# Seventeen completion waits at the end of a kernel, in GpSimd's program or in SyncE's

## The chip, the cores and the metric

The kernel runs on one core of one Trainium2 chip. The core has five engines with a program each: TensorE (PE, matrix products), VectorE (DVE), ScalarE (ACT), GpSimd (POOL) and SyncE (SP, which computes nothing; it issues transfers and waits). The engines meet only through semaphores: an instruction may wait until a semaphore has reached a value, and an instruction or a finished transfer may raise one. The metric is the device time of one launch in microseconds (us), as the median of several runs.

## What is computed

One block over 2048 tokens of width 448: a layer norm, a linear attention with 16 heads of 28 columns, a dense layer pair with a squared relu (448 to 1792 to 448), and a gate that joins the two. Inputs and output are bfloat16. Cut to its core:

```python
xn = _layernorm(x)
q, k, v = split(xn @ wqkv)                      # 16 heads of 28 columns
pq, pk = phi(q), phi(k)                         # where(t > 0, t + 1, exp(t)) + 1e-6
kv = einsum("bhsd,bhse->bhde", pk, v);  z = einsum("bhsd->bhd", pk)
s = (einsum("bhqd,bhde->bhqe", pq, kv) / (einsum("bhqd,bhd->bhq", pq, z) + 1e-6)) @ wo
r = relu(xn @ w1 + b1)
g = silu((r * r) @ w2 + b2)
return x + s * g
```

## The kernel before

The tokens stand in sixteen tiles of 128 rows. The kernel loads `x` and the weights, normalises the tiles, turns them on TensorE or by transfers, and then streams matrix products: keys, queries and the first dense layer tile by tile, then the token sums of the attention, the second dense layer (gate) and the attention's output. The result of a tile is put together in `gbuf` by VectorE and leaves with one transfer to `out`.

No engine's program is written down directly. `Program.add` collects operations with what they read and write; `schedule` puts them in an order for each engine, with durations that the code estimates; `emit` then writes each engine's program. For every operation `emit` works out which semaphores it has to wait for, and the inner function `body(h)` (made by `body_of(e)`) issues them in order: first `h.wait_ge(...)` for each wait, then the operation, which raises its engine's own semaphore by 1 or, when it is a transfer (`op.nbytes` is not 0), a semaphore of its own by 16.

Seventeen transfers write `out`: fourteen whole tiles (in `s_unit`, 112 KB each, twelve of them issued by SP and those of tiles 2 and 3 by ACT), and the last two tiles by `gate_last` (tile 14 whole by SP; tile 15 as a left part of 256 columns by ACT and a right part of 192 columns by SP, which is issued last of all). Line 429 is the helper `dma` that issues every transfer. Nothing in the kernel reads `out`, so something has to hold the launch open until the seventeen have landed. That is the loop at lines 297 to 300, at the end of `body`: one engine waits for each of the seventeen semaphores to reach 16. Line 295 is the wait that stands ahead of an operation anywhere else.

GpSimd has little to do here: it fills constants in the first 7.4 us (masks, an identity), and at line 1278 it scales a 128x64 piece of a weight. All its later candidates (the additions named `ad..`) were given to VectorE by the scheduler.

Of the kernel before, what the change touches and what calls it, by code (L numbers as in the profile page):

```python
# [46 lines left out]
class Program:  # L47
# [200 lines left out]
    def emit(self, nc, es):  # L248
        sems = {e: es.enter_context(nc.semaphore("q_" + e)) for e in self.ENGINES}
        n_dma = 0  # L250
        groups = {}
        for e in self.ENGINES:
            k = 0
            for op in self.order[e]:
                if op.group is not None:
                    if op.group not in groups:
                        groups[op.group] = es.enter_context(nc.semaphore(f"d{n_dma}")), ("d", n_dma)
                        n_dma += 1
                    op.sem, op.key = groups[op.group]
                    op.seq = 16 * sum(o.group == op.group for o in self.ops)  # L260
                elif op.nbytes:
                    op.sem, op.seq, op.key = es.enter_context(nc.semaphore(f"d{n_dma}")), 16, ("d", n_dma)
                    n_dma += 1
                elif op.label.startswith("table"):
                    op.sem, op.seq, op.key = es.enter_context(nc.semaphore(op.label)), 1, op.label
                else:
                    k += 1
                    op.sem, op.seq, op.key = sems[e], k, e
        done = {}
        waits = {}  # L270
        prev = {}
        for op in sorted(self.ops, key=lambda o: (o.start, 0 if o.eng == "pe" else 1)):
            e = op.eng
            known = dict(prev.get(e, {}))
            need = []
            deps = set(op.deps) | set(self.bankdeps.get(op, ()))
            deps.discard(op)
            for d in sorted(deps, key=lambda d: -d.end):
                if d.key == e == "pe" and d is not op.sync:
                    continue  # L280
                if known.get(d.key, 0) >= d.seq:
                    continue
                need.append((d.sem, d.seq))
                for kk, vv in done[d].items():
                    if known.get(kk, 0) < vv:
                        known[kk] = vv
                known[d.key] = max(known.get(d.key, 0), d.seq)
            waits[op] = need
            prev[e] = known
            done[op] = known  # L290
        def body_of(e):
            def body(h):
                for op in self.order[e]:
                    for s, v in waits[op]:
                        h.wait_ge(s, v)
                    op.emit(h, e).then_inc(op.sem, 16 if op.nbytes else 1)
                if e == "sp":
                    for o in self.ops:
                        if o.nbytes and o.writes and o.writes[0][0] == "out":
                            h.wait_ge(o.sem, 16)  # L300

            return body

        for e, h in (("sp", nc.sync), ("act", nc.scalar), ("pe", nc.tensor), ("dve", nc.vector), ("pool", nc.gpsimd)):
            body_of(e)(h)
# [1089 lines left out]
```

## Time and profile before

| what | value |
|---|---|
| time, median of 3 runs | 143.82 us (143.81 to 143.93) |
| the profiled execution: its own time | 144.04 us |
| the profiled execution: span from the program's first to its last instruction | 142.5 us |
| time outside the span | 1.54 us |
| TensorE busy | 138.5 us, 97% of the span |
| VectorE, ScalarE busy | 103.1 us, 79.0 us |
| GpSimd busy | 6.7 us, 40 instructions |
| granted TensorE clock | full in all slices |

The page lists the instructions of the program alone. Waits are instructions too (`EVENT_SEMAPHORE`); they are not counted as busy. A "q" behind an engine's name means its sequencer, that is waits and issued transfers. The trace also records every update of a semaphore with its time, before and after the program's own instructions; times here count from the first instruction of the program.

### The profile page before, as it was taken

The numbers are of one execution on the slowest core, as the hardware profiler recorded it, in microseconds if no ns is written. First come the engines' busy times: TensorE is split into PE (matmuls) and PEld (weight loads), VectorE is DVE, ScalarE is ACT, GpSimd is POOL, SyncE is SP. The second block draws the span as 40 slices with busy tenths as digits, with TensorE's granted clock in tenths as the row PEclk, the third lists the DMA queues.
The fourth block names the chain that finished last, engine by engine and source line by source line (L and its number), as shares of the span: only waits on it lengthen the run. The fifth ranks groups of instructions, "written<-read, shape, count | busy, mean of one in ns | idle before, by whom it ended". The sixth has DMA issues, their size and how long they took to land.

```text
span 142.5 us, 3235 instructions
## 1 busy us (share of the span) xinstructions
PE 138.5 (97%) x1300; PEld 71.2 (50%) x1300; DVE 103.1 (72%) x222; ACT 79.0 (55%) x146; POOL 6.7 (5%) x40
## 2 busy tenths in 40 slices
PE   7899999999999999999999999999999999999992
PEld 7854445454444544444544444435547455555472
DVE  2747999779689897789777799876035516874875
ACT  3578898040779626697863757787139430301412
POOL 7900001000000000000000000000000000000000
PEclk9999999999999999999999999999999999999999
DMA  4999994239933100233000000000686000223033
GB/s 94 312 302 292 338 293 78 44 49 270 212 42 49 20 0 0 46 50 47 9 5 0 0 0 5 0 0 18 155 223 145 1 0 17 93 88 101 32 97 97
DMA packets 23500, 12.91 MB, mean 91 GB/s; under 512 B 14274, under 2 KB 22718, under 8 KB 23486
## 3 DMA queue, kind: packets, MB, share of 16 engines
q1 hardware_dynamic: 21470, 11.17, 31.3%
q10 hardware_dynamic: 2016, 1.54, 4.7%
q8 instruction: 10, 0.16, 0.5%
q14 instruction: 4, 0.03, 0.1%
HBM read 9.23 MB, written 1.90 MB: 78 GB/s over the span
## 4 chain that ended last, share of the span: by engine, by line
PE 92%; DMA 3%; DVE 2%; SPq 1%; issue 0%
PE pb L780 29%; PE pb L1086 22%; PE pb L1178 7%; PE pb L881 7%; PE pb L723 7%; PE pb L733 6%; PE pb L1103 4%; DMA w_k<-in_A_wqkv_dram 3%; PE pb L1143 3%; PE pb L860 1%; DVE gbuf L1167 1%; PE pb L887 1%; PE pb L823 1%; PE pb L795 1%; PE pb L1030 1%; SPq L429 1%
## 5 line engine op out<-in xcount | busy, mean ns | idle before, releaser
L780 PE MATMUL pb<-xT,w 64*128 64x512 bf16 x378 | 43.6, 376 | 0.0
L1086 PE MATMUL pb<-w,r 64*128 64x448 bf16 x336 | 34.6, 349 | 0.0
L758 ACT ACTIVATE r<-pb,b1f 128x512 bf16<-128x512 f32 x40 | 25.7, 685 | 14.3 <-PE pb L780 13.9
L780 PEld LDWEIGHTS pb<-xT,w 64*128 64x128 bf16 x378 | 18.3, 94 | 21.8
L1086 PEld LDWEIGHTS pb<-w,r 64*128 64x128 bf16 x336 | 16.2, 94 | 16.0 <-issue 0.4
L770 ACT ACTIVATE r<-r 128x1024 bf16<-128x1024 bf16 x15 | 15.7, 1062 | 0.3
L755 DVE TENSOR_SCALAR r<-pb,b1f 128x512 bf16<-128x512 f32 x16 | 11.7, 745 | 4.1 <-PE pb L780 4.0
L1198 DVE TENSOR_TENSOR gbuf<-pb,gbuf 128x448 bf16<-128x448 f32 x14 | 8.1, 618 | 6.7 <-PE pb L1178 6.7
L490 DVE BATCH_NORM_STATS2 st<-x_tok 128x6 f32<-128x448 bf16 x16 | 9.6, 614 | 3.2 <-DMA x_tok<-in_A_x_dram 3.2
L723 PE MATMUL pb<-w_k,xT 64*128 64x448 bf16 x98 | 11.5, 349 | 0.0
L733 PE MATMUL pb<-xT,w_q 64*128 64x512 bf16 x84 | 11.0, 376 | 0.0
L1126 ACT ACTIVATE gbuf<-gbuf 128x448 bf16<-128x448 bf16 x14 | 7.0, 570 | 6.5 <-DVE gbuf L1076 5.9
L1178 PE MATMUL pb<-w_k,pqT 64*128 64x448 bf16 x96 | 10.6, 349 | 0.0
L1076 DVE TENSOR_TENSOR gbuf<-pb,b2b 128x448 bf16<-128x448 f32 x14 | 8.0, 614 | 3.4 <-PE pb L1086 2.0
L994 DVE TENSOR_TENSOR pqT<-pqT,xT 128x2048 bf16<-128x2048 bf16 x3 | 3.7, 1222 | 8.3 <-DMA xT<-scr 8.3
L713 DVE SCALAR_TENSOR_TENSOR pk<-pb,pk 128x448 bf16<-128x448 f32 x16 | 9.5, 617 | 0.2
L881 PE MATMUL pb<-pk,xn 128*128 128x448 bf16 x48 | 9.6, 353 | 0.0
L701 ACT ACTIVATE pk<-pb 128x448 bf16<-128x448 f32 x16 | 7.8, 543 | 3.1 <-PE pb L723 2.5
L701 ACT ACTIVATE pqT<-pb 128x512 bf16<-128x512 f32 x12 | 6.5, 597 | 4.9 <-PE pb L733 4.9
L769 DVE TENSOR_TENSOR r<-r 128x1024 bf16<-128x1024 bf16 x13 | 8.6, 685 | 0.1
L917 DVE TENSOR_TENSOR zacc<-zacc,pk 128x448 f32<-128x448 f32 x13 | 8.0, 618 | 0.1
L520 DVE TENSOR_SCALAR xn<-x_tok,mv,rstd 128x448 bf16<-128x448 bf16 x16 | 7.5, 500 | 0.6 <-ACT rstd L502 0.3
(98 smaller groups left out, 134.5 us busy)
## 6 DMA issues: line engine op xcount, KB each, us to landing
w<-in_B_w_dram SPq DMA_DIRECT2D x1, 1568.0 KB, 11.2
out_dram<-gbuf SPq DMA_DIRECT2D x13, 112.0 KB, 1.7
x_tok<-in_A_x_dram SPq DMA_DIRECT2D x3, 448.0 KB, 6.3
xT<-gbuf SPq DMA_DIRECT2D x32, 32.0 KB, 2.0
w<-in_B_w_dram SPq DMA_DIRECT2D x2, 384.0 KB, 6.3
xT<-scr SPq DMA_DIRECT2D x6, 112.0 KB
w<-in_B_w_dram SPq DMA_DIRECT2D x1, 576.0 KB, 5.8
xT<-scr ACTq DMA_DIRECT2D x5, 112.0 KB
```

The lines of the kernel that those rows point to most:

```text
L490: add("dve", lambda e, _: e.bn_stats(st6[:, si, :], x_tok[:, si, :]), [("x", si)], [("st", si)], 0.61, label=f"bn{si}").prio = hp(si, 0)
L701: "act", lambda e, _: e.activation(out=slot, in_=ps(buf)[0:rows, 0:n], func=AF.Exp), [buf, "actw"],
L713: lambda e, _: e.scalar_tensor_tensor(out=slot, in0=ps(buf)[0:rows, 0:n], scalar=1.0 + 1e-6, in1=slot, op0=ALU.add, op1=ALU.max),
L723: return e.matmul(ps(b)[:, 0:D], x_tile(rows, si, c), w_k[rows, c, :], start=start, stop=stop)
L733: return e.matmul(ps(b)[:, 0:512], w_q[rows, c, m * P : (m + 1) * P], x_group(rows, g, c), start=start, stop=stop,)
L755: return e.tensor_scalar(out=slot, in0=ps(b)[:, 0:512], scalar1=b1f[:, fi : fi + 1], scalar2=0.0, op0=ALU.add, op1=ALU.max)
L758: return e.activation(out=slot, in_=ps(b)[:, 0:512], func=AF.Relu, bias=b1f[:, fi : fi + 1])
L770: return e.activation(out=both, in_=both, func=AF.Square)
L780: return e.matmul(ps(b)[:, 0:512], w_1[rows, c, fi * P : (fi + 1) * P], x_group(rows, g, c), start=start, stop=stop,)
L881: last = e.matmul(ps(b)[:, 0:D], xn_cols(si, c * P, (c + 1) * P), pk[:, si, :], start=(si == 0), stop=(si == NT - 1),)
L1086: return e.matmul(ps(b)[:, 0:D], r_cols(rows, fi, si), w_2[rows, fi, :], start=start, stop=stop)
L1178: return e.matmul(ps(b)[:, 0:D], w, msb[rows, c, :], start=start, stop=stop)
```

## The change

One word in `emit`: the loop over the seventeen transfers is written at the end of GpSimd's program, and no longer at the end of SyncE's.

```diff
@@ -294,7 +294,7 @@
                     for s, v in waits[op]:
                         h.wait_ge(s, v)
                     op.emit(h, e).then_inc(op.sem, 16 if op.nbytes else 1)
-                if e == "sp":
+                if e == "pool":
                     for o in self.ops:
                         if o.nbytes and o.writes and o.writes[0][0] == "out":
                             h.wait_ge(o.sem, 16)
```

In the built program the seventeen waits are nine instructions in both kernels, with the same pairs in the same order: the first holds one wait, the other eight two each. The last two of the nine hold the wait for ACT's left part of tile 15 and, at the very end, that for SP's right part. On SP the nine stood behind the issue of the last transfer; on GpSimd they stand behind the scaling at line 1278. All other instructions are the same on each engine, in the same order.

## The prediction

> **What bounds the kernel now.** I read the page's busy times, then the chain that ended last in order of time, then the result transfers, then the waits of SP and GpSimd, and last the semaphore updates behind the program. The first view says that TensorE fills the span, so only what comes before its first or after its last product could be shortened or lengthened by other engines. The chain (start us, us, what) shows how the work ends.
>
> ```profile
> PE 138.5 (97%) x1300; PEld 71.2 (50%) x1300; DVE 103.1 (72%) x222; ACT 79.0 (55%) x146; POOL 6.7 (5%) x40
> ```
>
> ```profile
> 134.46 4.30 PE pb L1143 x28
> ...
> 140.16 0.48 DVE gbuf L1167 x2
> 140.65 0.02 issue
> 140.67 0.26 DVE gbuf L1167
> ```
>
> The last computation is VectorE's addition that ends at 140.93. From there to the span's end at 142.5 no engine computes: it is the last result transfer. Next are the lines of the result transfers (duration min/median/max in ns, first and last start in us), their issue to landing, and the nine wait instructions.
>
> ```profile
> L429 SPq DMA_DIRECT2D out_dram<-gbuf x14: 332/333/441, 120.1 to 141.0; - x14
> L429 ACTq DMA_DIRECT2D out_dram<-gbuf x3: 338/368/372, 125.7 to 140.5; - x3
> ```
>
> ```profile
> out_dram<-gbuf ACTq DMA_DIRECT2D x1, 64.0 KB, 1.6
> out_dram<-gbuf SPq DMA_DIRECT2D x1, 48.0 KB, 1.5
> ```
>
> ```profile
> L300 SPq EVENT_SEMAPHORE  x9: 17/28/28, 141.3 to 142.5; - x9
> ```
>
> ```profile
> SPq L300 <- DMA out_dram<-gbuf: 0.7, 2, 0.3
> ```
>
> SP issues the last transfer at 140.96 and is free of it at 141.29. Seven of the nine waits are already fulfilled and run through, some 60 ns apart, until 141.75. The eighth is held until ACT's 64 KB have landed at 142.08, the ninth until SP's 48 KB have landed: that semaphore's last update is at 142.45, the ninth wait starts at 142.47 and ends at 142.496, the end of the span. So the span ends with a transfer, and the engine that watches it adds 0.05.
>
> GpSimd's own lines show that it is free: its last work waits for a weight until 22.1 and ends at 22.8.
>
> ```profile
> POOL wqh L1278 <- DMA w_q<-in_A_wqkv_dram: 14.8, 1, 14.8
> ```
>
> ```profile
> 22.14 0.64 POOL L1278 TENSOR_SCALAR wqh<-w_q 128x64 bf16<-128x64 bf16 x1 [14.83 <-DMA w_q<-in_A_wqkv_dram]
> ```
>
> **What lies behind the span.** The profiled execution took 144.04, 1.54 more than its span. The semaphore updates in the trace show most of it. Semaphore 2, which no instruction of the kernel names, is raised nine times in a row at three places (us from the span's start):
>
> | place | 1 | 2 | 3 | 4 | 5 | 6 | 7 | 8 | 9 |
> |---|---|---|---|---|---|---|---|---|---|
> | ahead of the program | -0.370 | -0.336 | -0.298 | -0.254 | -0.230 | -0.118 | -0.080 | -0.045 | 0.001 |
> | first behind it | 140.186 | 141.103 | 141.141 | 141.184 | 142.604 | 142.649 | 142.687 | 142.721 | 142.768 |
> | second behind it | 143.558 | 143.592 | 143.630 | 143.674 | 143.698 | 143.796 | 143.834 | 143.869 | 143.915 |
>
> I read this as a barrier that goes through the five engines and back, PE, ACT, POOL, DVE, SP, DVE, POOL, ACT, PE. In the middle row the first update follows PE's last product (ended 139.98), the second ACT's last instruction (140.83), the fifth SP's last wait (142.496); POOL, done since 22.8, passes in 0.038 as soon as ACT has. In the top row the engines start the program in the order of the return: SP 0.000, DVE 0.122, POOL 0.135, ACT 0.139, PE 0.316. Between the two rows behind the program the other semaphores are written back, the last group (3 to 53) until 143.334, and the second pass begins 0.790 after the first has ended. So the time is: landing, the exit of the engine that watches it, the rest of the first pass behind that engine, then 0.790 + 0.357 for the reset and the second pass, and 0.12 that no record shows (144.04 - 143.915).
>
> **The change part by part.**
>
> *Taken from SP:* nine waits. Seven cost nothing, as they ran between 141.29 and 141.75 under ACT's landing at 142.08; without that cover they would cost 7 x 0.060 = 0.42, and that is all a shorter SP queue could ever have given. SP now reaches its exit at 141.29 plus its exit time of 0.108 (142.496 to 142.604), some 141.4, and waits in the barrier. No transfer starts sooner, since the nine stood behind the last of them.
>
> *Added to GpSimd:* the same nine. The first holds its engine from 22.8 to the landing at 131.96; the others pass as their transfers land. Behind them on GpSimd stands nothing of the kernel, ahead of them nothing that is late; what waits for them is the barrier. On waking: GpSimd's one wait for a transfer (line 295, at 21.932) began 24 ns after the update, SP's two began 17 ns after theirs: +0.007. The end of the span moves by no more.
>
> *The exit, from the end of the last wait to the engine's update.* SP's took 0.108. GpSimd's is not in this trace, since it passed long ago. From below: its start barrier shows a semaphore instruction of 17 ns whose update came 25 ns after its start, so 0.008 at least, a gain of 0.100. From above: ACT took 0.276 (140.827 to 141.103), a loss of 0.168; farther still, GpSimd's own way into the program, 0.135 to its update at 0.630, is 0.495, a loss of 0.387. I take 0.160: two semaphore instructions of GpSimd stand 78 ns apart where SP's stand 60, so SP's 0.108 becomes 0.140, and GpSimd's drain at the start ended 50 ns after the last memset, of which I count 0.020 since there is nothing to drain. That is +0.052.
>
> [...]
>
> *The rest of the pass.* GpSimd's update is the third, SP's the fifth. With SP last, the rest was 142.768 - 142.604 = 0.164. With GpSimd last, DVE, SP, and the way back must follow one after the other, and that is what the other two rows show from 3 to 9: 0.299 (-0.298 to 0.001) and 0.285 (143.630 to 143.915). The difference is +0.121 to +0.135; I take +0.128. It is more than two short hops because the step from 5 to 6 takes 0.112 or 0.098 when DVE has only just passed, and took 0.045 when it stood ready.
>
> [...]
>
> *The sum:* 0.007 + 0.052 + 0.128 = +0.19 us. Against the profiled execution that is 144.04 + 0.19 = 144.23. That execution lay 0.22 above the median of the runs shown, and nothing in the sum depends on it, so the forecast is 143.82 + 0.19 = 144.01, slower by 0.13%. I take 0.2%, here 0.29 us, as what a measurement of this kernel can tell from no change, so this counts as within it.
>
> **The rivals.**
>
> 1. *GpSimd leaves slowly.* The same chain, but an exit as long as ACT's 0.276 or up to its 0.495 at the start. Then the sum is 0.007 + 0.168 + 0.128 = +0.30, up to +0.007 + 0.387 + 0.128 = +0.52: 144.12 to 144.34, slower by 0.2% to 0.4%. It decides from an exit of 0.26 on, where the sum passes 0.29. For it: ACT and PE (0.206) both left more slowly than SP, and GpSimd is slower than SP in its semaphore steps. Against it: GpSimd is idle then, and in its rows of the start a drain and memsets stand in the 0.495.
> 2. *The order of arrival costs nothing.* If the nine updates are a count and not a chain in that order, the last engine's place doesn't matter: the +0.128 falls away and the exit alone is left, -0.10 to +0.05, so 143.72 to 143.88, not slower beyond the measure. For it: a count would be raised as well. Against it: four updates wait in line with engine ends, and POOL, done at 22.8, raised nothing before 141.14.
> 3. *Faster by more than 0.29.* SP would need work of that size behind its waits that now runs under the landing. All that the trace has there is the 0.108 exit. Only the 0.12 without records could hide more.
> 4. *The change does not do what it says*, SP still ending last: the time stays at 143.82. Nothing in SP's program is left to wait for a landing, so I count this with 2.
>
> **How the numbers follow.** Forecast 0.53, with its own range 143.90 to 144.10; rival 1 0.36; rivals 2 and 4 0.07; rival 3 0.04. Faster 0.04. Within 0.2%: 0.53 + 0.07 = 0.60. Slower 0.36. The range starts in rival 2 at 143.76 and ends with rival 1's upper bound, 144.34.
>
> **What would show it.** Nine waits of line 300 on GpSimd's sequencer, the last ending within 0.05 of 142.5; in the first row of updates behind the program the third (not the fifth) following the last wait, by 0.16 in the forecast and 0.26 or more in rival 1, and then 0.29 to the ninth. The second pass should again begin 0.79 later and take 0.36. If the fifth comes at about 142.6 and the ninth 0.16 after, rival 2 is right. If the span itself moves by more than 0.1, my first step, that the watching engine does not set the landing, is wrong.

## The result, and the profile after

| | before | changed |
|---|---|---|
| median of 5 runs | 143.81 us (143.64 to 143.93) | 144.33 us (144.20 to 144.61) |
| profiled execution: its own time | 144.04 us | 144.26 us |
| its span | 142.5 us | 142.1 us |
| its time outside the span | 1.54 us | 2.19 us |

The ratio is 1.0041, with a 95% interval of 1.0027 to 1.0056: slower by 0.39 to 0.81 us. The prediction had +0.19 us.

The span is no longer than it was; it scatters from 141.8 to 143.5 us between executions of the kernel before. Time minus span scatters far less, and the tables below use it: its mean is 1.55 us in 91 executions of the kernel before, made beside the experiments (1.49 to 1.62), and 2.13 us in five of the changed one (2.10 to 2.16). The spans of single executions are on record to 0.1 us, which alone makes a scatter of 0.05 us either way. All of the loss, 0.58 us, lies outside the span. Disturbed executions (a granted clock of 0.987 or 0.988) are left out of all means, and as the profiled one of the two executions with a memset (experiment 10) was such a one, only what stands behind its last wait is read.

First the end of the chain that ended last in the changed kernel (start us, us, what; pieces between are left out).

```profile
134.01 4.30 PE pb L1143 x28
...
140.20 0.02 issue
140.22 0.26 DVE gbuf L1167
```

Each piece is as long as before; the whole stands 0.45 us earlier. Next the transfers of the results in the changed kernel: the issue's duration in ns and its place, then size and time to landing.

```profile
L429 SPq DMA_DIRECT2D out_dram<-gbuf x14: 332/333/446, 119.6 to 140.5; - x14
L429 ACTq DMA_DIRECT2D out_dram<-gbuf x3: 338/367/371, 125.2 to 140.0; - x3
```

```profile
out_dram<-gbuf ACTq DMA_DIRECT2D x1, 64.0 KB, 1.6
out_dram<-gbuf SPq DMA_DIRECT2D x1, 48.0 KB, 1.5
```

Issue and landing are the same too: from the last issue (140.509) to its landing (142.006) it is 1.50 us, as it was (1.49). The next line shows the waits, by the view of their line in the changed kernel (duration min/median/max in ns, first and last start):

```profile
L300 POOLq EVENT_SEMAPHORE  x9: 17/43/43, 131.5 to 142.0; - x9
```

They stand on GpSimd's sequencer (POOLq). The first starts at 131.5, when the first of its transfers has landed, and the last at 142.030, 24 ns after its semaphore's last update. A wait for two semaphores takes GpSimd 43 ns where SP took 28. Together the last wait ends 0.067 us after the landing, against 0.045: +0.022 inside the span, and so no reason for the loss.

Now the updates of semaphore 2 in the trace of the changed kernel, the same three rows as in the prediction (the trace of either kernel has a fourth, which ends 2.4 us ahead of the program):

| place | 1 | 2 | 3 | 4 | 5 | 6 | 7 | 8 | 9 |
|---|---|---|---|---|---|---|---|---|---|
| ahead of the program | -0.370 | -0.336 | -0.298 | -0.254 | -0.230 | -0.119 | -0.080 | -0.046 | 0.000 |
| first behind it | 139.707 | 140.652 | 142.605 | 142.649 | 142.672 | 142.769 | 142.808 | 142.842 | 142.889 |
| second behind it | 143.678 | 143.712 | 143.750 | 143.794 | 143.817 | 143.914 | 143.953 | 143.987 | 144.034 |

The third update is late now, not the fifth: the row stops between ACT and POOL. From the end of GpSimd's last wait (142.073) to the third update it takes 0.532 us, where SP needed 0.108 to its fifth. From there to the ninth it is 0.284 in place of 0.164. The stretch to the second pass (0.789) and that pass (0.356) are what they were (0.790 and 0.357).

| step, us | before | changed | difference |
|---|---|---|---|
| end of the last wait to the engine's own update | 0.108 | 0.532 | +0.424 |
| from there to the ninth update | 0.164 | 0.284 | +0.120 |
| reset and second pass | 1.147 | 1.145 | -0.002 |
| sum behind the last wait | 1.419 | 1.961 | +0.542 |

In these two executions time minus span differs by 0.64 us, so that 0.10 of it stands in no record; over all executions it differs by 0.58, which leaves 0.04.

### The profile page after: what moved, and what is told of

Same layout as the page of the kernel before. It is cut to its first block, busy times and chain, and to the rows that moved or that the text cites. A ratio compares the mean times of both kernels' runs of the same rounds, so it can differ in the third digit from the quotient of the medians.

```text
span 142.1 us, 3235 instructions
## 1 busy us (share of the span) xinstructions
PE 137.6 (97%) x1300; PEld 70.4 (50%) x1300; DVE 103.0 (73%) x222; ACT 79.2 (56%) x146; POOL 6.7 (5%) x40
## 3 DMA queue, kind: packets, MB, share of 16 engines
q10 hardware_dynamic: 2016, 1.54, 4.7%
## 4 chain that ended last, share of the span: by engine, by line
PE 96%; DVE 2%; ACT 1%; issue 0%
PE pb L780 29%; PE pb L1086 22%; PE pb L1178 7%; PE pb L881 7%; PE pb L723 7%; PE pb L733 6%; PE pb L1103 4%; PE pb L1143 3%; PE pb L1213 3%; PE pb L860 1%; DVE gbuf L1167 1%; PE pb L887 1%; PE pb L823 1%; PE pb L795 1%; PE pb L1030 1%; PE pb L597 1%
```

## The experiments

All are edits of the loop at lines 297 to 300. In what follows, the watcher is the engine that holds the wait for the last result to land; exit is the time from the end of its last wait to its own update of semaphore 2; rest is from there to the ninth update. Exit and rest are from one profiled execution each, time minus span is the mean over a kernel's executions. The diffs show only the lines that matter.

**1. GpSimd waits for sixteen, SP for the last one.**

```diff
-                if e == "sp":
-                    for o in self.ops:
-                        if o.nbytes and o.writes and o.writes[0][0] == "out":
-                            h.wait_ge(o.sem, 16)
+                outs = [o for o in self.ops if o.nbytes and o.writes and o.writes[0][0] == "out"]
+                for o in {"pool": outs[:-1], "sp": outs[-1:]}.get(e, []):
+                    h.wait_ge(o.sem, 16)
```

> GpSimd waits for sixteen results, SP for the last one alone. Theory (what counts is which engine sees the last landing, and how far it stands from the end of the barrier): SP is last again, so the tail from the end of its last wait to the ninth update is 0.108 + 0.164 = 0.27 us and the time is that of before, within 0.1 us. GpSimd's last wait ends 0.37 us before SP's and its exit is 0.53 us, so GpSimd's update (the third) comes about 0.1 us after SP's last wait has ended: the tail grows by that and by the way from the third to the ninth update, to some 0.5 us, if it is really late; if its exit is shorter when another engine is last, the tail is 0.27. Rival (any waits for results on GpSimd cost 0.5 us): as the changed kernel, 0.5 us slower than before, with a tail of 0.8 us.

The lines of the waits in this kernel:

```profile
L299 POOLq EVENT_SEMAPHORE  x8: 43/43/43, 132.3 to 142.1; - x8
L299 SPq EVENT_SEMAPHORE  x1: 17/17/17, 142.4 to 142.4; - x1
```

GpSimd's last wait ends at 142.115 and its update, the third, comes at 142.648, 0.533 later. SP's last wait had ended at 142.453. So the third update comes 0.195 after SP's wait is over, later than SP's own exit of 0.108 needs, and SP has to wait for GpSimd, although GpSimd had been released by the landing 0.37 us before the last. The ninth update is at 142.933, 0.480 after SP's last wait; time minus span is 1.80 us (1.73 to 1.86), between the two kernels, and the ratio 1.0021 (1.0008 to 1.0033). The wait on GpSimd costs as much as its exit reaches past SP's, which is the theory's second case, and not the 0.5 us of the rival.

**2. SP waits for sixteen, GpSimd for the last one.**

```diff
+                for o in {"sp": outs[:-1], "pool": outs[-1:]}.get(e, []):     # the rest as in experiment 1
```

> SP waits for sixteen results, GpSimd for the last one alone, with one wait instruction. Theory (exit of the last engine plus the rest of the barrier): as the changed kernel, exit 0.53 us and rest 0.285 us, so 0.5 us slower than before. Rival (each wait on GpSimd adds its part, or GpSimd's exit grows with what it waited for): eight of nine instructions are gone, so at most 0.1 us slower than before.

```profile
L299 SPq EVENT_SEMAPHORE  x8: 28/28/28, 140.9 to 141.6; - x8
L299 POOLq EVENT_SEMAPHORE  x1: 17/17/17, 142.0 to 142.0; - x1
```

Ratio 1.0047 (1.0031 to 1.0063), time minus span 2.09 us (2.05 to 2.15). GpSimd has one wait instruction of 17 ns; its exit is 0.538, the rest 0.285. The number of waits plays no part.

**3, 4 and 7. All seventeen on VectorE, on ScalarE, on TensorE.**

```diff
-                if e == "sp":
+                if e == "dve":        # and "act", "pe"
```

> All seventeen waits at the end of VectorE's program. Theory: VectorE is fourth in the barrier, the rest from the fourth to the ninth update is 0.241 us (0.077 more than with SP), and its exit is between SP's 0.108 and ACT's 0.276 us: 0.08 to 0.25 us slower than before. Rival 1 (only GpSimd leaves slowly and order costs nothing): 0 to 0.17 us. Rival 2 (any engine but SP leaves as slowly as GpSimd): exit 0.5 us, 0.5 us slower.

> All seventeen waits at the end of ScalarE's program, behind its last transfer. Theory: ACT is second in the barrier, the rest from the second to the ninth update is 0.323 us, and its exit was 0.276 us in the kernel before: 0.276 + 0.323 = 0.60 us from the end of the last wait to the ninth update against 0.27 with SP, so 0.33 us slower. Rival 1 (order costs nothing): 0.17 us slower. Rival 2 (any engine but SP leaves as slowly as GpSimd): exit 0.53 us, 0.58 us slower.

> All seventeen waits at the end of TensorE's program. Theory (chain PE, ACT, POOL, DVE, SP and back): PE is first, so the rest from the first to the ninth update is the whole pass, 0.357 us, and with an exit of 0.206 us the tail from the end of the last wait to the ninth update is 0.56 us against 0.27 with SP: 0.29 us slower, time minus span 1.85 us. All of the first row's nine updates come after the last wait. Rival (order costs nothing): 0.10 us slower. Rival (all engines but SP leave as GpSimd does): 0.53 + 0.357, 0.62 us slower.

The waits of the three kernels, in this order, each by the view of its line:

```profile
L300 DVEq EVENT_SEMAPHORE  x9: 21/49/50, 140.8 to 142.6; - x9
```

```profile
L300 ACTq EVENT_SEMAPHORE  x9: 17/38/38, 140.5 to 142.2; - x9
```

```profile
L300 PEldq EVENT_SEMAPHORE  x9: 51/51/51, 138.0 to 142.2; - x9
```

| watcher | its update | exit | rest | exit + rest | time minus span | ratio to before |
|---|---|---|---|---|---|---|
| SP (before) | 5th | 0.108 | 0.164 | 0.27 | 1.55 (1.49 to 1.62) | |
| DVE | 4th | 0.141 | 0.240 | 0.38 | 1.67 (1.62 to 1.73) | 1.0022 (1.0011 to 1.0034) |
| POOL (changed) | 3rd | 0.532 | 0.284 | 0.82 | 2.13 (2.10 to 2.16) | 1.0041 (1.0027 to 1.0056) |
| ACT | 2nd | 0.177 | 0.322 | 0.50 | 1.46 (1.43 to 1.49) | 0.9997 (0.9981 to 1.0012) |
| PE | 1st | 0.186 | 0.357 | 0.54 | 1.81 (1.76 to 1.85) | 1.0017 (1.0002 to 1.0032) |

The rest grows from SP back to PE, in the order PE, ACT, POOL, DVE, SP, and in each kernel just the update in the table is the first that comes after the last wait. That settles the chain and excludes the count. The exits say that GpSimd is alone: all others leave in 0.11 to 0.19 us behind a wait. (Behind an issued transfer ScalarE took longer, 0.276 us in the kernel before and 0.275 in the changed one.) By time minus span, DVE (+0.12 us) and PE (+0.26 us) agree with exit + rest (+0.11 and +0.27). ACT does not: its updates add up to +0.23, its time minus span came out 0.10 us below that of the kernel before. The updates are where they should be (the last one of the second pass at 143.84), but the time (143.65 in the profiled execution) is shorter by about 0.33 us than the records add up to. Experiments 8, 11 and 12 are on this.

**5. GpSimd waits for fourteen, SP for three.**

```diff
+                for o in {"pool": outs[:14], "sp": outs[14:]}.get(e, []):
```

> GpSimd waits for the fourteen whole-tile results of tiles 0 to 13, SP for the last three. The last of the fourteen landed at about 139.9 us, so with an exit of 0.53 us GpSimd could raise its update at 140.4, before ACT's at 141.1. Theory (the watcher costs only if its exit makes the barrier wait): no cost; time minus span 1.55 us as in the kernel before, first pass after SP's last wait 0.27 us, third update 0.04 us after the second. Rival (waits on GpSimd cost as such): time minus span near 2.1 us, or at least the 1.8 us of the split with sixteen waits.

```profile
L299 POOLq EVENT_SEMAPHORE  x7: 42/43/43, 130.3 to 140.1; - x7
L299 SPq EVENT_SEMAPHORE  x2: 17/22/28, 142.3 to 142.7; - x2
```

GpSimd's last wait ends at 140.155, the third update follows the second after 0.039 (141.323 to 141.362): its exit is covered. From SP's last wait to the ninth update it is 0.289. Ratio 1.0007 (0.9982 to 1.0032): no cost that the time can tell. Time minus span is 1.62 us (1.57 to 1.66), 0.06 us above the kernel before, which the theory did not have.

**6 and 10. One more instruction on GpSimd behind the waits: a drain, or a memset.**

```diff
                             h.wait_ge(o.sem, 16)
+                    h.drain()                          # experiment 6
+                    h.memset(junk[:, :], 0.0)          # experiment 10; junk is a tile of 128x1
```

> The changed kernel with one drain instruction on GpSimd behind its nine waits, to see in the profile what a drain costs there when nothing is under way. Theory 1 (the exit's 0.53 us is mostly such a drain after long idleness): the drain's record lasts 0.3 us or more, and the exit behind it shrinks to some 0.2 us, sum unchanged. Theory 2 (the 0.53 us are GpSimd's own way out, no drain of work): the drain is short, 0.05 to 0.2 us, the exit behind it stays at 0.53 us and the time grows by about what the drain takes.

> The changed kernel with one memset of 128x1 on GpSimd behind its nine waits, into a tile that nothing reads. Theory 1 (GpSimd's 0.53 us from its last instruction to its update are fixed, whatever came last): from the memset's end to the third update again 0.45 to 0.55 us. Theory 2 (the exit is long because GpSimd's cores had been idle since 22 us and must be woken): the memset itself is late or long (0.1 us at the start of the program), and the exit behind it falls to 0.1 to 0.3 us.

The drain of experiment 6, then the memset of experiment 10, each by the view of its line:

```profile
L301 POOLq DRAIN  x1: 41/41/41, 142.2 to 142.2; - x1
```

```profile
L303 POOL MEMSET junk<- x1: 99/99/99, 144.8 to 144.8; 128x1 f32 x1
```

In both kernels the seventeen waits are eight instructions of two each, and the last one, for a transfer that landed 20 us before, stands on the added instruction. The drain takes 41 ns, shorter than either theory had it, and from its end (142.192) to the third update (142.716) it is 0.524. The ratio of experiment 6 is 1.0057 (1.0026 to 1.0088), its time minus span 2.15 us (2.11 to 2.19). The memset takes 99 ns, as at the start of the program, starts 0.070 after the last wait, and from its end (144.864) to the third update (145.376) it is 0.512. So the half microsecond is neither a drain of work nor a waking of an idle engine: it is nearly the same behind a wait, a drain or an operation (0.51 to 0.54).

**8, 9, 11 and 12. Idle waits that only make a program longer.** Nine wait instructions on input transfers that landed long ago, at the end of another engine's program:

```diff
+                if e == "act":        # experiments 8 and 11; "pool" in 9; twice over in 12
+                    for o in [o for o in self.ops if o.nbytes and o.group is None][:17]:
+                        h.wait_ge(o.sem, 16)
```

Experiments 8, 9 and 12 are edits of the kernel before, 11 of the changed one.

> The kernel before, with seventeen waits on SP, and nine more wait instructions at the end of ScalarE's program, on input transfers that landed long ago, so that they hold nothing back. With the waits for the results on ScalarE the time came out 0.35 us below what the updates of the barrier add up to, and a block of 8 KB of instructions was fetched at 142.84 us that no other kernel fetches. Theory (ScalarE's program, longer by nine instructions, moves what stands behind it, and the end of the timed stretch with it, whatever the waits are for): time minus span 1.2 us, 0.35 us faster than before, with the same fetch of 8 KB. Rival (it comes from ScalarE being the last engine to leave): 1.55 us and no change.

> The kernel before, with SP's seventeen waits, and nine more wait instructions at the end of GpSimd's program, on input transfers that landed long ago. GpSimd's program has the length it has in the changed kernel, but it leaves at about 24 us. Theory (the 0.54 us come from GpSimd leaving last, by its exit and its place): no cost, time minus span 1.55 us. Rival (GpSimd's longer program moves something behind the program, as ScalarE's does): time minus span differs from 1.55 by 0.1 us or more.

> The changed kernel, waits on GpSimd, with the nine idle wait instructions at the end of ScalarE's program that took 0.30 us off the kernel before. Theory (the two effects are apart: GpSimd's exit and place cost 0.54 us before the barrier's end, ScalarE's longer program takes 0.30 us off behind it): time minus span 2.13 - 0.30 = 1.83 us. Rival (ScalarE's longer program only helps when SP leaves last): 2.1 us.

> The kernel before, with seventeen idle wait instructions at the end of ScalarE's program in place of the nine tried first. Theory (what counts is that ScalarE's program passes the end of a block of instructions, once): time minus span 1.25 us as with nine, 0.30 us less than before, and again one fetch of 8 KB near 142.7. Rival (each additional instruction takes its share off): 1.0 us. Rival 2 (chance of where the program ends): back at 1.55 us.

| experiment | waits for results | made longer | time minus span | ratio to before |
|---|---|---|---|---|
| 8 | SP | ACT by 9 | 1.25 (1.21 to 1.29) | 0.9984 (0.9963 to 1.0005) |
| 12 | SP | ACT by 17 | 1.33 (1.27 to 1.38) | 0.9986 (0.9962 to 1.0010) |
| 9 | SP | POOL by 9 | 1.62 (1.56 to 1.67) | 1.0004 (0.9988 to 1.0021) |
| 11 | POOL | ACT by 9 | 2.17 (2.12 to 2.22) | 1.0052 (1.0030 to 1.0074) |

Experiment 9 is a control for the change: GpSimd's program is as long as in the changed kernel, leaves at 22.8, and the cost is 0.06 us by time minus span, as in experiment 5; the ratio can't tell it from none. So of the changed kernel's 0.58, some 0.54 is the chain and about 0.04 may come with the longer program alone.

Experiment 8 shows that ScalarE's missing 0.3 us also comes off when ScalarE waits for no result: nine more instructions do it. Their number is not the whole of it, as experiment 11 has them too and gains nothing. The queue through which instructions are fetched shows one fetch more in experiment 8 (first line) than in the kernel before (second line):

```profile
q14 instruction: 5, 0.04, 0.1%
```

```profile
q14 instruction: 4, 0.03, 0.1%
```

That fetch, 8 KB at 142.73, is also in experiments 4, 11 and 12. But it is not the cause by itself: in experiment 11 it is there (142.11) and the time gains nothing. The barrier's updates do not show the gain: the profiled execution's time minus its last update is 0.125 us in the kernel before, 0.196 in experiment 11, and -0.19 to -0.20 in experiments 4, 8 and 12. Where the timed stretch begins and ends is in no record here, so what the 0.3 us are stays open. That seventeen instructions took less off than nine is in the records: ScalarE then left just ahead of SP (141.88 and 141.98), and the tail from SP's last wait to the last update is 1.52 us in place of 1.42. The kernels of experiments 8 and 12 have the shortest times of all here (medians 143.67 and 143.60 against 143.81 and 143.89 beside them), yet both intervals include no change.

## Why the prediction was off

*What bounds the kernel, and the span: right.* The last landing ends the span with either watcher, and the nine waits cost nothing in it. The sign named against this step, a span that moves by more than 0.1 us, did occur (142.50 to 142.07), but it could decide nothing: the spans of the kernel before alone differ by 1.7 us. The steps from the last issue to the landing and from there to the end of the last wait show it. Waking was 24 ns against 17, as taken from line 295; the longer wait instruction (43 against 28 ns) was left out and is worth 0.015.

*Nothing to gain from a shorter SP queue: right.* SP's last instruction ended at 140.84 and SP's update still came fifth, 0.067 after GpSimd's.

*The rest of the pass: right.* Predicted +0.121 to +0.135, measured +0.120, and the order of the engines was confirmed by five watchers. The hops are not equal here: behind the third update of the changed kernel they took between 0.023 (from the fourth to the fifth) and 0.097 (from the fifth to the sixth).

*The exit: wrong in size, and nearly the whole of the error.* The step read "I take 0.160", +0.052, between a lower bound of 0.008 and an upper one of 0.495. Measured was 0.532 in the changed kernel, +0.424, and 0.512 to 0.538 in the five kernels in which GpSimd saw the last landing: above even the farther bound. That is 0.37 us more than the sum had. The other terms of the sum are off by 0.015 and -0.008, and the part without records, taken as unchanged at 0.12, may have grown by some 0.04. The mistake was in the reasoning from near rows: I scaled SP's exit by the spacing of semaphore instructions and reckoned that an idle engine has little to do. Experiments 6 and 10 (0.524 and 0.512) show that it hardly depends on which instruction came last. The row that was nearly right, GpSimd's own 0.495 on its way into the program, was called the farther one. GpSimd's 0.532 against SP's 0.108 says that one engine's exit can't be used to price another's.

*The rivals.* Rival 1, GpSimd leaves slowly, is what happened, and the time of 144.33 lies at the top of its 144.12 to 144.34. That it lies inside is luck, as the exit was longer than the rival's longest: with the three terms as measured (0.022, 0.424 and 0.120) its sum would be 144.39. The rival had a chance of 0.36 and should have had more than the forecast. Rival 2 (a count) and rival 4 fell with the third update, rival 3 with the slower time: nothing of SP's was hidden. Its remark that the part without records could hide more was sound, as experiments 4, 8 and 12 moved that part by 0.3 us.

What GpSimd does in its half microsecond is not in any record here. That it comes again in every kernel in which the barrier had to wait for GpSimd is shown (0.51 to 0.54 us in six kernels, experiment 1 among them), why it is so long is not.

## What to carry to other kernels

The engine that holds the last completion wait also sets when the end barrier can go on, so the choice has a price although the span does not show it: exit plus the rest of the chain, 0.27 us on SP, 0.38 on DVE, 0.50 to 0.54 on ACT and PE, 0.82 on GpSimd. On ACT the measured time did not pay that price, for a reason that stays open. In this kernel that says to leave the last landing to SP, and not to GpSimd (0.58 us more outside the span). Early ones were waited for on GpSimd at no cost that the time can tell (experiment 5, ratio 1.0007), where its last wait ended 1.2 us before ScalarE's update; from the exit of 0.51 to 0.54 us I estimate that 0.54 us would do. When a change touches the end of a program, compare time minus span and the semaphore updates behind the last instruction, and price an engine's way out by that engine's own rows, not by another's.

## What was not expected of the hardware

- A wait for two fulfilled semaphores takes 28 ns on SP, 38 on ACT, 43 on GpSimd, 49 on DVE and 51 on PE; for one it takes 17 on SP, ACT and GpSimd, 21 on DVE and 51 on PE.
- GpSimd needs 0.51 to 0.54 us from its last instruction to its update of the barrier, behind a wait, a drain or a memset alike; the other four need 0.11 to 0.19 behind a wait, and ScalarE 0.28 behind an issued transfer.
- Nine idle instructions at the end of ScalarE's program took 0.30 us off the time outside the span without a gain in the updates of the barrier, seventeen took 0.23 us off, and nine took nothing off when GpSimd left last. The cause is open.
- With seven or nine more instructions on GpSimd the time outside the span was 0.06 us longer, though the engine had long left or its exit was covered (experiments 9 and 5). The cause is open. The stretch between the two passes was 0.82 in place of 0.79 us in both, but so it was in experiments 1, 3, 6 and 12 too, and not in the changed kernel.
